# Softmax of a windowed attention: exponentials and sums taken for 512 columns at a time, on three engines

## The chip, the cores and the metric

The kernel runs on one core of a Trainium2 chip. The metric is device time in microseconds (us) of one execution. Five engines with a queue each work side by side: TensorE (PE, with its weight loads as PEld), VectorE (DVE), ScalarE (ACT), GpSimd (POOL) and SyncE (SP), which here issues all DMAs. Every queue runs in order.

## What is computed

```python
# q, k, v: (8, 8, 576, 64) float32
scores = np.matmul(q, k.transpose(0, 1, 3, 2)) / np.sqrt(64)
mask = (rel >= 0) & (rel < 64)           # rel: query position minus key position
scores = np.where(mask, scores, -1e9)
scores = scores - np.max(scores, axis=-1, keepdims=True)
attn = np.exp(scores)
attn = attn / (np.sum(attn, axis=-1, keepdims=True) + 1e-09)
x = np.matmul(attn, v)                   # turned to (4608 tokens, 512)
out = np.maximum(x @ w_in, 0) ** 2 @ w_out   # w_in (512, 2048), w_out (2048, 512)
```

## The kernel before

The 4608 tokens are cut into 12 tiles of 384. Each tile's attention is done in 3 **sections** of four blocks of 64 queries for two heads, 36 sections in all, numbered from 0. A section's scores lie as 128 partitions by 512 columns: eight groups of 64 columns, and each group is one softmax row per partition. The feed-forward part follows; with its high and low parts of every operand it is nearly all of the TensorE's work.

The function `section` (line 224) issues a section's steps; a letter names each:

- S: scores on TensorE (line 238). o: ScalarE copies one half of them to SBUF (line 246). s: VectorE puts the other half under the mask (lines 255, 256). z: VectorE takes the negated maxima of the eight groups (line 258).
- y: multiplies the eight maxima by the scale (line 260), on VectorE (`d`) or GpSimd (`p`).
- e and f: eight exponentials on ScalarE (line 266), four in each letter, of 64 columns each. The scale and, as bias, the group's negated maximum go with the instruction, and it also gives the group's sum; the profile shows each as an ACTIVATE and an ACTIVATION_READ_ACCUMULATOR.
- k: adds the epsilon to the sums (line 269). R: their reciprocals on VectorE (line 272). m: the probabilities times them, 128x512 (line 275), on GpSimd but for section 0.
- X: transposes on TensorE (line 279). x: VectorE masks them into SBUF (line 283). V: the product with v on TensorE (line 301). H and Q: high and low part of its result, on ScalarE (line 316) and VectorE (line 318).

The order of the instructions has two makers. The first ten sections (0 to 9) stand with all other work of their time in a list written out by hand, the string `order` (lines 491 to 510); a token is a letter, a number and, for some, an engine letter. Sections 0 to 5 lie at the kernel's start, 6 to 9 later. In the same string the steps a, b, c, d, h, l (`weight`, line 110) split one block of the weights into high and low part: a and h on ScalarE (lines 121, 132), b (two instructions, lines 123 and 124), c, d (lines 126, 128) and l (line 135) on VectorE. M (line 407), r and p (line 416 on), g, G (lines 424, 426) and O (line 449) are a feed-forward step: the first product, its evacuation and square, high and low part, the second product. T and U turn q and k on TensorE, t and u copy them, K fills TensorE with products of no use.

The 26 later sections are ordered by `Plan` (lines 655 to 723): each operation is given to it with an engine, a cost and what it reads and writes. TensorE's order is as written; the others are placed by when they are due. `weigh` (line 785) gives it the softmax:

```python
plan("dve", 0.68, by(section, "z", i), [sel], [nm])
plan("dve", 0.07, by(section, "y", i, "d"), [], [nm])
plan("act", 1.4, by(section, "e", i), [nm], [sel, sums])
plan("act", 1.4, by(section, "f", i), [nm], [sel, sums])
```

k and R follow there on VectorE and m on GpSimd; `cross` (line 817) plans X and x. Plain GpSimd work beside it is `mix` (lines 539, 543) and the squares (line 970).

## Time and profile before

| | |
|---|---|
| Three runs | 839.74, 839.88 and 840.94 us, median 839.88 |
| Span of the profiled execution, first to last instruction | 841.0 us; the page gives no other time for it |
| Busy share of the span | PE 98%, PEld 91%, VectorE 74%, ScalarE 52%, GpSimd 29% |
| Mean granted TensorE clock | 0.998 of full speed |

A page of the profile lists busy times, waits and the chain of work that ended last; the trace answers for a stretch, a line or an engine. Times in a timeline are us from the span's start. A matmul's duration is that of a pipelined instruction: matmuls overlap each other, so their busy sums, not their means, say what they take. An instruction on VectorE, ScalarE or GpSimd also overlaps the next one of its engine by up to a tenth of a us.

### The profile page before, as it was taken

The page shows a single profiled execution, that of the slowest core. Times are in us where ns is not written, and L with a number is a line of the kernel's source. Part 1 is how long each engine was busy: PE and PEld are TensorE (multiplying, and loading weights), DVE is VectorE, ACT ScalarE, POOL GpSimd, SP SyncE. Part 2 cuts the span into 40 slices and gives each one's busy share as a digit, 9 for nine tenths or more (in the row PEclk, how much of TensorE's full clock was granted, in tenths as well). Part 3 has the DMA queues.
Part 4 walks back from the last instruction along what each step waited for, and adds up shares of the span by engine and source line. Part 5 has one row for each costly group of instructions (what it writes and reads, how often), then busy time and mean ns, then how long its engine had stood idle before and what let it go on. Part 6 is the DMA issues. An engine that isn't in the chain of part 4 may idle for free.

```text
span 841.0 us, 18284 instructions
## 1 busy us (share of the span) xinstructions
PE 826.7 (98%) x6928; PEld 764.2 (91%) x6928; DVE 620.5 (74%) x908; ACT 435.2 (52%) x1181; POOL 242.7 (29%) x313
## 2 busy tenths in 40 slices
PE   8799999999999999999999999999999999999998
PEld 6689899889999999999999999999999999999997
DVE  5899998467666867867777866788766759566876
ACT  6796774655546554544452455444355424455441
POOL 1220003024547520221251334252233452202121
PEclk9999999999999999999999999999999999999999
DMA  9999964737588894999896897999895866789842
GB/s 211 223 321 301 288 272 80 146 101 183 148 196 258 219 186 101 308 258 215 184 315 211 219 229 169 252 292 223 275 309 140 262 202 192 244 269 310 243 167 76
DMA packets 292264, 184.99 MB, mean 220 GB/s; under 512 B 191184, under 2 KB 257488, under 8 KB 290128
## 3 DMA queue, kind: packets, MB, share of 16 engines
q1 hardware_dynamic: 292176, 183.81, 78.6%
q8 instruction: 55, 0.90, 0.5%
q14 instruction: 33, 0.27, 0.1%
HBM read 142.87 MB, written 40.89 MB: 219 GB/s over the span
## 4 chain that ended last, share of the span: by engine, by line
PE 90%; DVE 3%; SPq 3%; ACT 2%; issue 1%; DMA 1%; POOL 0%; ACTq 0%; POOLq 0%
PE banks L940 26%; PE banks L1038 24%; PE banks L449 13%; PE banks L407 13%; PE banks L1189 5%; PE banks L238 4%; PE banks L301 3%; PE banks L279 2%; SPq L160 1%; ACT a L121 1%; DVE a L126 1%; SPq L188 1%; DMA w<-in_k_dram 1%; ACT sel L266 1%; SPq L107 1%
## 5 line engine op out<-in xcount | busy, mean ns | idle before, releaser
L1038 PE MATMUL banks<-w 128*128 128x512 f32 x888 | 199.8, 381 | 0.0
L1038 PEld LDWEIGHTS banks<-w 128*128 128x128 f32 x888 | 165.9, 189 | 21.6
L407 PE MATMUL banks<-x,w 128*128 128x384 f32 x768 | 137.9, 329 | 0.4 <-ACT r L416 0.4
L449 PE MATMUL banks<-w,g 128*128 128x512 f32 x576 | 136.1, 382 | 0.0
L407 PEld LDWEIGHTS banks<-x,w 128*128 128x128 f32 x768 | 125.9, 189 | 5.7 <-ACT r L416 2.3
L940 PE MATMUL banks<-x,w 128*128 128x384 f32 x768 | 130.3, 326 | 0.0
L940 PEld LDWEIGHTS banks<-x,w 128*128 128x128 f32 x768 | 125.6, 189 | 0.0
L449 PEld LDWEIGHTS banks<-w,g 128*128 128x128 f32 x576 | 106.4, 189 | 13.3 <-issue 0.3
L266 ACT ACTIVATE sel<-sel,nm 128x64 f32<-128x64 f32 x272 | 90.8, 336 | 22.3 <-DVE nm L260 21.9
L940 PE MATMUL banks<-w 128*128 128x384 f32 x576 | 100.7, 329 | 0.0
L970 POOL TENSOR_TENSOR g<-g 128x384 f32<-128x384 f32 x48 | 46.5, 973 | 180.5 <-ACT g L981 172.6
L940 PEld LDWEIGHTS banks<-w 128*128 128x128 f32 x576 | 93.4, 189 | 1.6
L1045 DVE TENSOR_TENSOR w<-w,banks 128x512 f32<-128x512 f32 (+1 forms) x61 | 41.1, 677 | 41.3 <-PE banks L1038 41.2
L416 ACT ACTIVATE r<-banks 128x384 f32<-128x384 f32 x64 | 31.2, 487 | 65.3 <-PE banks L407 59.9
L275 POOL TENSOR_TENSOR sel<-sel,nm 128x512 f32<-128x512 f32 x33 | 37.3, 1131 | 81.9 <-ACT g L981 31.9
L539 POOL TENSOR_TENSOR a<-w 128x256 f32<-128x256 f32 x28 | 24.4, 887 | 104.9 <-DVE w L135 75.0
L426 DVE TENSOR_TENSOR g<-r,g 128x384 fp32r<-128x384 f32 x64 | 38.2, 600 | 21.3 <-ACT g L424 14.4
L1022 ACT CAST w<-w 128x512 fp32r<-128x512 f32 x37 | 23.0, 621 | 56.3 <-PE banks L1038 56.3
L266 ACT ACTIVATION_READ_ACCUMULATOR sel<-sel,nm 128x1 f32 x272 | 51.1, 188 | 0.0
L283 DVE TENSOR_TENSOR pt<-banks,masks 128x1024 f32<-128x1024 f32 x33 | 40.2, 1219 | 9.1 <-PE banks L279 9.1
L958 DVE TENSOR_TENSOR w<-banks,r 128x384 f32<-128x384 f32 x64 | 38.3, 598 | 11.7 <-PE banks L940 11.2
L421 DVE TENSOR_TENSOR r<-r 128x384 f32<-128x384 f32 x38 | 24.7, 650 | 26.3 <-ACT r L416 26.2
(167 smaller groups left out, 1273.4 us busy)
## 6 DMA issues: line engine op xcount, KB each, us to landing
w<-mixed SPq DMA_DIRECT2D x128, 256.0 KB, 5.6
w<-kept SPq DMA_DIRECT2D x114, 256.0 KB, 6.1
w<-kept SPq DMA_DIRECT2D x52, 512.0 KB, 7.3
kept<-w SPq DMA_DIRECT2D x16, 1024.0 KB, 8.7
vt<-in_v_dram SPq DMA_DIRECT2D x144, 64.0 KB, 3.7
w<-in_moe_w_in_dram SPq DMA_DIRECT2D x16, 512.0 KB, 7.7
w<-in_moe_w_out_dram SPq DMA_DIRECT2D x16, 512.0 KB, 7.8
raw<-in_q_dram SPq DMA_DIRECT2D x112, 72.0 KB, 2.9
```

What stands on the lines that cost most here:

```text
L266: act.activation(sels[i][:, w, hd], sels[i][:, w, hd], AF.Exp, bias=nms[i][:, n], scale=SCALE, accum_out=sums[i][:, n])
L275: (dve if eng == "d" else pool).tensor_tensor(p, p, rs[i][:, :, None].broadcast_to([P, SW * 2, QB]), ALU.mult)
L283: dve.tensor_tensor(pts[i].rearrange("p (w n) q -> p w n q", n=2), ps_t[i][:, :, None, :].broadcast_to([P, SW, 2, P]), masks.rearrange("p ...
L407: pe.matmul(h_ps, lhsT=weights(kk, part), rhs=in_turn(x[xx][:, kk // 2, kk % 2]), start=n == 0, stop=n == 3 * NK - 1)
L426: (pool if eng == "p" else dve).tensor_tensor(gs[n][1], rg.pop(n), gs[n][0].bitcast(F32), ALU.subtract)
L449: pe.matmul(acc(t, tb), lhsT=gg[:, tb * P:(tb + 1) * P], rhs=in_turn(weights(part)), start=f == 0 and n == 0, stop=f == NF - 1 and n == 2)
L940: pe.matmul(ps[:, :TT], lhsT=w[:, part, kk * P:(kk + 1) * P], rhs=in_turn(x[:, xx, kk]), start=n < 4 and m == 0, stop=m == 5, skip_group_c ...
L958: plan("dve", 0.6, lambda: dve.tensor_tensor(to(), ps, other(), ALU.add), [kps, ko], keys, 0, after)
L970: plan("pool", 0.95, lambda: pool.tensor_tensor(x(), x(), x(), ALU.mult), [], keys)
L1038: pe.matmul(ps[:, :DM // parted], lhsT=gg[:, m // 2, m % 2], rhs=in_turn(wo_slot(w[m])[:, part, cols]), start=m == 0 and n == 0, stop=m == ...
L1045: plan("dve", 0.72 / parted, lambda ps=ps, to=to: dve.tensor_tensor(by_half(to()), by_half(to()), ordered(ps[:, :DM // parted]), ALU.add), ...
L1189: pe.matmul(ps[:, x * 2 * P:(x + 1) * 2 * P], lhsT=gg[:, st, x * P:(x + 1) * P], rhs=in_turn(w[:, st, part]), start=c == 0, stop=c == 5, s ...
```

## The change

Three of a section's steps are made anew. y adds the negated maxima to all 512 columns, by an addition with a broadcast operand of the same shape as m's multiplication; in `order` all y stand on GpSimd now, and the planner is told GpSimd too. e is one exponential of 512 columns with the scale, without bias and without a sum. f is a sum over each group of 64 on VectorE, a reduction of the shape of z's. In `order` the tokens y0d and y1d become y0p and y1p, and for sections 2, 3, 4, 6, 7 and 9 the letters e and f change places, so that e stands first. The planner's costs change with the steps.

```diff
--- before.py
+++ after.py
@@ -257,14 +257,12 @@
         elif op == "z":
             dve.tensor_reduce(nms[i], sels[i].rearrange("p w h c -> p (w h) c"), AX.X, ALU.max, negate=True)
         elif op == "y":
-            (dve if eng == "d" else pool).tensor_scalar(nms[i], nms[i], SCALE, None, ALU.mult)
-        elif op in "ef":
-            for w in range(SW // 2):
-                w += "ef".index(op) * SW // 2
-                for hd in range(2):
-                    n = slice(2 * w + hd, 2 * w + hd + 1)
-                    act.activation(sels[i][:, w, hd], sels[i][:, w, hd], AF.Exp, bias=nms[i][:, n], scale=SCALE,
-                                   accum_out=sums[i][:, n])
+            p = sels[i].rearrange("p w h c -> p (w h) c")
+            (dve if eng == "d" else pool).tensor_tensor(p, p, nms[i][:, :, None].broadcast_to([P, SW * 2, QB]), ALU.add)
+        elif op == "e":
+            act.activation(sels[i], sels[i], AF.Exp, scale=SCALE)
+        elif op == "f":
+            dve.tensor_reduce(sums[i], sels[i].rearrange("p w h c -> p (w h) c"), AX.X, ALU.add)
         elif op == "k":
             (dve if eng == "d" else pool).tensor_scalar(sums[i], sums[i], EPS, None, ALU.add)
         elif op == "R":
@@ -489,11 +487,11 @@
             n1 += 1
     steps += [(0, f) for f in range(n0, NF)] + [(2, f) for f in range(LAG)]
     order = """
-        L0 K5 P0 L1 P1 T1 t1d T0 t0a J0 j0 Y0 S0 o0a T2 t2a s0 z0 y0d T3 t3d J1 L2 K2 S1 j1 e0 o1a T4 t4a v0 w1 Y1 L3 v1
-        N0 f0 K2 T5 d0 k0p t5a h0 s1 K5 z1 y1d S2 R0 m0d e1 l0 o2a X0 K5 x0 V0 s2 f1 k1p T6 R1 w2 z2 a1 b1 m1p X1 H0a Q0
-        c1 t6a v2 L4 N1 y2p K2 f2 T7 t7a x1 S3 e2 d1 U0 o3a s3 V1 k2p R2 u0a U1 z3 h1 u1a K5 H1a l1 Q1
-        m2p X2 x2 w3 v3 a2 b2 K3 c2 y3p f3 V2 T8 T9 H2a Q2 t8a t9a d2 S4 e3 o4a k3d R3 h2 s4 M0 U2 r0 u2a l2 p0a v4 z4
-        U3 u3a a3 m3p X3 x3 b3 g0 G0 M1 c3 r1 p1a y4p S5 o5a w4 v5 s5 d3 f4 e4 w5 w6 g1 G1 V3 H3a k4p R4 z5 Q3
+        L0 K5 P0 L1 P1 T1 t1d T0 t0a J0 j0 Y0 S0 o0a T2 t2a s0 z0 y0p T3 t3d J1 L2 K2 S1 j1 e0 o1a T4 t4a v0 w1 Y1 L3 v1
+        N0 f0 K2 T5 d0 k0p t5a h0 s1 K5 z1 y1p S2 R0 m0d e1 l0 o2a X0 K5 x0 V0 s2 f1 k1p T6 R1 w2 z2 a1 b1 m1p X1 H0a Q0
+        c1 t6a v2 L4 N1 y2p K2 e2 T7 t7a x1 S3 f2 d1 U0 o3a s3 V1 k2p R2 u0a U1 z3 h1 u1a K5 H1a l1 Q1
+        m2p X2 x2 w3 v3 a2 b2 K3 c2 y3p e3 V2 T8 T9 H2a Q2 t8a t9a d2 S4 f3 o4a k3d R3 h2 s4 M0 U2 r0 u2a l2 p0a v4 z4
+        U3 u3a a3 m3p X3 x3 b3 g0 G0 M1 c3 r1 p1a y4p S5 o5a w4 v5 s5 d3 e4 f4 w5 w6 g1 G1 V3 H3a k4p R4 z5 Q3
         h3 l3 a4 M2 r2 p2a O0 b4 O1 w7 v6 m4p X4 x4 c4 M3 g2 G2 V4 y5p e5 f5 k5p r3 H4a p3a g3 R5 d4 h4 a5 Q4
         w8 O2 G3 l4 m5p X5 x5 M4 a6 V5 w9 w10 w11 i3 r4 p4a g4 b6 H5d Q5 b5 M5 I3 r5 p5a c6 d6 w12 M6 w13 G4 O4
         h6 g5 r6 p6a c5 g6 M7 w14 d5 h5 w15 v7 v8 G5 O5 l6 r7 p7a a8 q0 M8 G6 O6 g7 l5 a7 r8 M9 b8 c8 d8 h8 G7 r9 O7
@@ -503,10 +501,10 @@
         B5 B6 B7 l12 G15 M17 r17 a14 p17a O15 M18 G16 O16 b13 c13 r18 M19 d13 b14 g17 G17 O17 c14 h13 p18a l13
         g18 G18 O18 d14 r19 M20 a15 p19a b15 g19 G19 h14 l14 r20 O19 c15 d15 p20a g20 M21 G20 B8 B9 D0 q2 O20 h15 l15 r21
         M22 p21a g21 G21 O21 D1 q3 r22 p22d g22 M23 r23 G22 O22 p23d M24 g23 G23 O23 Z22 S6 D2 q4 r24
-        p24d g24 G24 o6a M25 D3 s6 O24 S7 z6 r25 p25a g25 G25 M26 r26 p26d D4 y6p O25 M27 g26 W22 q5 G26 o7d O26 f6
-        e6 k6p R6 v9 s7 r27 p27a M28 q6 m6p r28 p28a z7 y7p f7 S8 g27 D5 q7 M29 X6 G27 O27 o8a x6 s8 z8 g28 V6
-        r29 v10 p29a g29 e7 M30 H6a G28 Q6 G29 S9 O28 k7p y8p e8 R7 m7p X7 o9d x7 r30 s9 p30d f8 k8p R8 m8p M31
-        r31 z9 y9p V7 g30 H7a Q7 G30 p31d g31 O29 X8 x8 O30 V8 f9 e9 G31 i31 k9p R9 m9p H8a Q8 D6 M32 r32 I31 Z31 v11
+        p24d g24 G24 o6a M25 D3 s6 O24 S7 z6 r25 p25a g25 G25 M26 r26 p26d D4 y6p O25 M27 g26 W22 q5 G26 o7d O26 e6
+        f6 k6p R6 v9 s7 r27 p27a M28 q6 m6p r28 p28a z7 y7p e7 S8 g27 D5 q7 M29 X6 G27 O27 o8a x6 s8 z8 g28 V6
+        r29 v10 p29a g29 f7 M30 H6a G28 Q6 G29 S9 O28 k7p y8p e8 R7 m7p X7 o9d x7 r30 s9 p30d f8 k8p R8 m8p M31
+        r31 z9 y9p V7 g30 H7a Q7 G30 p31d g31 O29 X8 x8 O30 V8 e9 f9 G31 i31 k9p R9 m9p H8a Q8 D6 M32 r32 I31 Z31 v11
         W31 D7 p32d g32 X9 M33 x9 G32 r33 p33d g33 G33 q8 q9"""
     ps_f = {}
 
@@ -789,9 +787,9 @@
         plan("act", 0.56, by(section, "o", i), ["s_ps"], [sel])
         plan("dve", 0.73, by(section, "s", i), ["s_ps"], [sel])
         plan("dve", 0.68, by(section, "z", i), [sel], [nm])
-        plan("dve", 0.07, by(section, "y", i, "d"), [], [nm])
-        plan("act", 1.4, by(section, "e", i), [nm], [sel, sums])
-        plan("act", 1.4, by(section, "f", i), [nm], [sel, sums])
+        plan("pool", 1.13, by(section, "y", i, "p"), [nm], [sel])
+        plan("act", 0.65, by(section, "e", i), [], [sel])
+        plan("dve", 0.68, by(section, "f", i), [sel], [sums])
         if i in loads:
             b, part = divmod(loads[i], len(VPARTS))
             if b < B:
```

## Rows read from the trace of the kernel before

**Rows 1.** The page's first part: busy us (share of the span) xinstructions of each engine.

```profile
PE 826.7 (98%) x6928; PEld 764.2 (91%) x6928; DVE 620.5 (74%) x908; ACT 435.2 (52%) x1181; POOL 242.7 (29%) x313
```

**Rows 2.** Windows: busy us (xinstructions) of PE, PEld, DVE, ACT, POOL; PEclk; DMA; GB/s.

```profile
20.00:30.00 10.00, 6.30 (x133) 4.96 (x134) 8.40 (x12) 7.56 (x27) 4.14 (x6) 0.99 0.81 211
30.00:40.00 10.00, 9.01 (x124) 8.37 (x123) 8.13 (x11) 7.33 (x25) 0.03 (x1) 0.84 1.00 217
40.00:50.00 10.00, 9.21 (x126) 8.46 (x126) 9.57 (x14) 9.42 (x29) 1.59 (x4) 1.00 0.98 287
50.00:60.00 10.00, 8.71 (x92) 7.51 (x91) 9.58 (x13) 9.78 (x27) 4.38 (x4) 1.00 1.10 324
80.00:90.00 10.00, 10.00 (x54) 9.00 (x53) 9.83 (x13) 8.03 (x12) 0.00 (x0) 1.00 0.58 103
200.00:330.00 130.00, 130.00 (x1217) 119.80 (x1216) 90.33 (x143) 69.03 (x227) 62.35 (x92) 1.00 0.77 191
31.00:32.00 1.00, 1.00 (x7) 1.00 (x6) 0.65 (x1) 1.00 (x2) 0.00 (x0) 0.50 1.11 166
```

**Rows 3.** Waits of PE, whole span: us in total, times, longest us.

```profile
PE banks L279 <- POOL sel L275: 1.3, 1, 1.3
PE banks L301 <- DVE pt L283: 1.2, 2, 0.6
...
PE banks L407 <- ACT r L416: 0.4, 1, 0.4
```

**Rows 4.** Groups by line, each form apart: busy us, mean ns of one, idle before.

```profile
L266 ACT ACTIVATE sel<-sel,nm 128x64 f32<-128x64 f32 x272 | 90.8, 336 | 22.3 <-DVE nm L260 21.9 <-POOL nm L260 0.2
L266 ACT ACTIVATION_READ_ACCUMULATOR sel<-sel,nm 128x1 f32 x272 | 51.1, 188 | 0.0
...
L258 DVE TENSOR_REDUCE nm<-sel 128x8 f32<-128x512 f32 x34 | 23.0, 678 | 0.7
...
L1022 ACT CAST w<-w 128x512 fp32r<-128x512 f32 x37 | 23.0, 621 | 56.3 <-PE banks L1038 56.3
...
L123 DVE TENSOR_SCALAR a<-a 128x1024 f32<-128x1024 f32 x15 | 10.8, 720 | 1.6 <-ACT a L121 1.6
...
L275 DVE TENSOR_TENSOR sel<-sel,nm 128x512 f32<-128x512 f32 x1 | 0.7, 691 | 0.0
```

**Rows 5.** Timeline of POOL: start us, us, instruction, idle before it and releaser.

```profile
21.27 1.04 POOL L275 TENSOR_TENSOR sel<-sel,nm 128x512 f32<-128x512 f32 x1 [0.32 <-DVE nm L272]
...
29.40 0.24 POOL L260 TENSOR_SCALAR nm<-nm 128x8 f32<-128x8 f32 x1
...
50.91 1.21 POOL L260 TENSOR_SCALAR nm<-nm 128x8 f32<-128x8 f32 x1
...
56.87 2.02 POOL L275 TENSOR_TENSOR sel<-sel,nm 128x512 f32<-128x512 f32 x1 [0.39 <-DVE nm L272]
...
176.28 1.04 POOL L275 TENSOR_TENSOR sel<-sel,nm 128x512 f32<-128x512 f32 x1 [4.04 <-DVE nm L272]
```

**Rows 6.** Timeline of DVE, 20 to 60 us.

```profile
21.79 1.08 DVE L123 TENSOR_SCALAR a<-a 128x1024 f32<-128x1024 f32 x1
...
30.42 1.23 DVE L135 TENSOR_TENSOR w<-a,w 128x1024 fp32r<-128x1024 f32 x1 [1.48 <-ACT w L132]
...
50.81 1.21 DVE L135 TENSOR_TENSOR w<-a,w 128x1024 fp32r<-128x1024 f32 x1
...
53.31 1.22 DVE L283 TENSOR_TENSOR pt<-banks,masks 128x1024 f32<-128x1024 f32 x1
...
56.63 1.36 DVE L128 SCALAR_TENSOR_TENSOR a<-w,a 128x1024 int32<-128x1024 int32 x1
```

**Rows 7.** Timeline of PE, around 55 us and at 178 us.

```profile
54.59 0.93 PE L301 MATMUL banks<-pt,vt 64*64 64x64 f32 x48
...
58.94 0.65 PE L279 MATMUL banks<-ident,sel 128*128 128x128 f32 x4 [1.29 <-POOL sel L275]
...
178.04 0.63 PE L279 MATMUL banks<-ident,sel 128*128 128x128 f32 x4
```

## The prediction

> **What bounds the kernel now.** I read the page's first part before anything else: TensorE is busy for 826.7 us of 841.0, so at most 841.0 - 826.7 = 14.3 us can be won by anything that TensorE waits for, however much a softmax shrinks on another engine [rows 1]. The question is then where these 14.3 us lie, and the windows answer it. From 200 to 330 us TensorE is busy 130.00 of 130, while VectorE has 90.33 and ScalarE 69.03: a burst of sections there costs nothing, and relief of ScalarE there gives nothing. At the start it is otherwise: TensorE has 6.30, 9.01, 9.21 and 8.71 of 10 in the four windows from 20 to 60 us, and from then on 10.00 again [rows 2]. The list of waits says what it waits for there: the transposes X wait 1.3 us once for GpSimd's m, V 1.2 us in all for VectorE's x, and a product once 0.4 us for ScalarE [rows 3].
>
> So the start decides, and there sections 0 to 5 share their engines with the splitting of the weights. Look at who is full: from 40 to 60 us VectorE has 9.57 and 9.58, ScalarE 9.42 and 9.78. VectorE stays at 9.83 from 80 to 90, where ScalarE has fallen to 8.03 [rows 2]. Two full engines alternate on the chain; the change unloads one and loads the other.
>
> **The change, part by part.** The sum is made against the profiled execution: 841.0 us from first to last instruction, the only time that the page gives for it, 1.1 above the median 839.88 of the three runs. I work out a difference and add it to the median.
>
> *Exponentials.* Eight activations of 64 columns with accumulator reads go. They take between 8 x 0.336 = 2.7 us, if the reads hide behind the next activation, and 8 x (0.336 + 0.188) = 4.2 us if they do not. The new one is not in the trace; the nearest row is a ScalarE operation of 512 columns, 0.62 us, the bounds are 0.34 (one of 64 columns) and 0.69 (VectorE's price for 512) [rows 4]. I take 0.62: ScalarE wins 2.1 to 3.6 us a section. What is that worth? Only where TensorE waits for ScalarE, 0.4 us in all [rows 3], or where VectorE waits for it.
>
> *Sums.* f is a reduction of z's shape, 0.68 us [rows 4]: six sections before 60 us, 6 x 0.68 = 4.1 us more in VectorE's queue. Room there is the idle time from 20 to 60 us: 1.60 + 1.87 + 0.43 + 0.42 = 4.3 us [rows 2], of which the largest piece is 1.48 us ahead of a weight step [rows 6]. About 0.4 of it are waits inside a softmax that stay, since k still stands on GpSimd behind the sum; I take 3.9. By itself the reduction would nearly fit, were it spread as the idle time is. It is not: of the 4.3 only 0.85 lie behind 40 us, where f3 to f5 need 3 x 0.68 = 2.0, so 1.2 us is what the sums alone cost.
>
> *Subtractions on GpSimd.* y grows from 0.24 us to the shape of m, 1.04 us [rows 5]. Its own length is the smaller part. Look at the two engines side by side. At 50.91 a GpSimd y of eight columns takes 1.21 us in place of 0.24, and it ends at 52.12, just behind VectorE's weight step that runs from 50.81 to 52.02. At 56.87 an m takes 2.02, beside a VectorE step that runs to 57.99: 0.98 more. At 21.79 it goes the other way: VectorE's b takes 1.08 us in place of 0.72, beside an m that began first, at 21.27, and ends at 22.31 [rows 4 to 6]. Whichever began first holds the other off. So a subtraction of 1.04 us can hold up VectorE for 1.04 us where its next step is a weight step or m.
>
> The Trainium skill states this as a rule (SBUF — State Buffer, "SBUF: two separate sides"): GpSimd and VectorE share one port pair under an exclusive lock for a whole instruction, when VectorE runs a 2-port mode or has two SBUF inputs. By it the sum below holds, without it the second rival's; this trace agrees, with the 1.21 and 2.02 us above.
>
> I go through the queues in the new order. y0 starts when z0 ends; a copy from PSUM passes it, then a half b waits some 0.4 us. y1 starts when z1 ends, R0 passes, and m0 waits some 0.9 us. y2 stands behind m1 on GpSimd and slips in between the two instructions of b1: 1.04. Everything is then so late that m2 meets l1: 0.65. y3 and y4 fall beside Q and x steps, which read PSUM and one SBUF operand; no row shows these held up, so I take zero, with 1.04 each as the bound. y5 waits for l3, as before, but then takes its turn before b4: 1.04. Together 0.4 + 0.9 + 1.04 + 0.65 + 1.04 = 4.0 us; the bounds are zero and 6 x 1.04 + 0.65 = 6.9.
>
> *The start's sum.* VectorE gets 4.1 + 4.0 us and has 3.9 of room: its step l4 and section 5's m come 4.2 us later. Who waits? V of section 4 stands right behind x (x ends at 53.31 + 1.22 = 54.53, V starts at 54.59), and X of section 5 right behind m (56.87 + 2.02 = 58.89, X at 58.94) [rows 5 to 7]. There is no slack, and behind them TensorE has no idle time to take the delay up [rows 2]. Moving the two old y off VectorE gives back too little to count.
>
> The skill's GPSIMD Engine Reference (4.1, Engine selection) also speaks against y: two-input elementwise work is about twice as slow there as on VectorE, which with VectorE's 0.69 would make 1.4 us an estimate for y and the sum above some 0.3 us longer for each y that holds VectorE. The row of the same shape says 1.04 [rows 5], a factor of 1.5, and decides.
>
> *Sections 6 to 9.* In section 8 f stands between p30 and R in VectorE's queue, where R once followed at once: 0.68 for f and some 0.4 for k on GpSimd and the two hand-overs, 1.1 us. m ended at 176.28 + 1.04 = 177.32 and X starts at 178.04 [rows 5, 7], so 0.7 are slack and 0.4 us is lost. The other three have longer cover or a shorter chain.
>
> *The 26 planned sections* I cost at nothing. A section's chain loses 2.1 or more on ScalarE and gains 0.9 on GpSimd and 0.7 on VectorE; VectorE, 90.33 of 130, and GpSimd, 62.35 of 130, have room for it [rows 2]. The cover is the time between a section's m and its X; where a collision takes it away, that section costs up to 1 us, and a new order by the planner's new costs can bring more such places.
>
> *The clock.* TensorE's granted clock is 0.50 from 31 to 32 us, its lower level of 1.2 GHz, after a window in which it was busy 6.30 of 10; the window 30 to 40 has 0.84, which is 1.6 us lost of 10 [rows 2]. The later arrival of V1 and X1 may fill that idle time, and new waits of about 2 us ahead of V4 and X5 may open another. I take zero and keep 1.6 us for either end.
>
> Sum: 4.2 + 0.4 = 4.6, so 839.9 + 4.6 = 844.5 us.
>
> **Rivals.** *ScalarE was the bound.* The time between two VectorE steps at 40 to 56 us could be ScalarE's: it has 9.42 and 9.78 of 10 there. Then sections 4 and 5 come early by 2.1 us each, X5's 1.3, V's 1.2 and the 0.4 us wait vanish [rows 3], and the time is 839.9 - 2.9 = 837.0. The point from which it decides: VectorE would have to have 2 us of room from 40 to 60, and has 0.85. Chance 0.14.
>
> *The collisions cost little*, because VectorE's steps happen to fall otherwise than in my walk. Then the sums' 1.2 and section 8's 0.4 are left, less what the clock gives back: 839.9 + 1.6 = 841.5 at most, and about 841 as its centre. For it: y3 and y4 already cost nothing in my count. Against it: weight steps fill VectorE's queue in this stretch, and b, d and l are the very ones that show a collision in the rows [rows 5, 6]. Chance 0.22.
>
> *The middle breaks too.* Ten of the later sections lose 0.4 us each, as section 8 does: 844.5 + 4 = 848.5. For it: GpSimd at half its time in the window from 200 to 330. Against it: TensorE waits for nothing there. Chance 0.08, within slower.
>
> **How the numbers follow.** About 0.2% (1.7 us) is what a measurement of this kernel can tell from no change: 838.2 to 841.6. Forecast 0.56 and the third rival 0.08 make slower 0.64; the second rival makes same 0.22, the first faster 0.14. The forecast's own bounds: with no collision 841.5; with all of them 4.1 + 6.9 - 3.9 = 7.1, + 0.4 + 1.6 = 9.1, so 849.0. The range goes from 839.0 to 849.0: its low end takes in the second rival even where the clock gives all its 1.6 back (839.9), and a last us for my walk through the queues; left out are the first rival and what lies above.
>
> **What would show it.** Right: VectorE at 9.8 or more of 10 from 20 to 60 us; b1, m0 and b4 longer by about a subtraction; X5 at about 63 us with a wait for GpSimd of 2 us; no wait of TensorE behind 200 us; ScalarE's busy time down by 36 x 2.1 = 76 us or more without a gain. Wrong: X5 at or before 59 us, no longer weight steps beside y, or waits of TensorE in the middle.

## The result and the profile after

The changed kernel takes 851.31 us in the median of four runs (850.3 to 852.55), beside 839.87 (839.74 to 840.94) for the kernel before on the same chip: a ratio of 1.0132 with a 95% interval of 1.0118 to 1.0146. It is slower, as forecast, but by 11.4 us where 4.6 were forecast, and it lies above the range.

The page's first part for the changed kernel, in the columns of [rows 1]:

```profile
PE 828.6 (98%) x6928; PEld 765.0 (90%) x6928; DVE 639.5 (75%) x916; ACT 363.4 (43%) x641; POOL 279.7 (33%) x341
```

ScalarE does 71.8 us less than before, VectorE 19.0 more, GpSimd 37.0 more. The span is 848.7 us, 7.7 longer: TensorE stands idle for 20.1 us where it was 14.3, which is 5.8 of them, and its own busy time is 1.9 longer. (The span of before is that of an untypical execution, as shown below; a typical one is some 3 us shorter.)

The windows of the changed kernel, in the columns of [rows 2]:

```profile
20.00:30.00 10.00, 6.56 (x136) 5.24 (x138) 9.61 (x13) 4.54 (x7) 2.96 (x4) 1.00 0.90 219
30.00:40.00 10.00, 7.67 (x133) 6.80 (x123) 9.93 (x13) 5.05 (x8) 3.92 (x3) 0.80 0.93 215
40.00:50.00 10.00, 9.54 (x121) 8.81 (x122) 8.24 (x13) 7.44 (x14) 2.08 (x2) 0.86 1.03 308
50.00:60.00 10.00, 9.02 (x93) 8.10 (x92) 9.84 (x13) 5.84 (x9) 3.50 (x3) 1.00 1.10 324
60.00:70.00 10.00, 8.17 (x87) 6.88 (x86) 9.18 (x14) 6.37 (x9) 2.15 (x2) 1.00 1.06 375
200.00:330.00 130.00, 128.07 (x1206) 117.90 (x1206) 92.28 (x143) 52.72 (x107) 75.79 (x107) 1.00 0.80 189
```

Set against [rows 2], VectorE is full in three of the four windows from 20 to 60 us, ScalarE is far from full in all of them, TensorE now also idles in the window behind 60, and the stretch from 200 to 330 us, which had none, now has 1.93 us. In this execution TensorE's clock also fell: it has 0.50, the level of 1.2 GHz, from 36 to 42 us, behind a wait of 1.49 us ahead of section 2's V. At half its clock it came to the transposes X3 at 44.72 us (42.52 in the repeat of this kernel, **after_again** below, whose clock is 1.00 there), and VectorE's next x waited 1.66 us for them: that is why VectorE has 8.24 in the window behind. The wait alone does not tell when the clock falls: the repeat has the same 1.49 us ahead of the same V.

The list of waits of the changed kernel (us in total, times, longest), answering to [rows 3]; L277 is X, L299 is V, L405 a feed-forward product, L273 is m, L281 is x, L414 is r:

```profile
PE banks L277 <- POOL sel L273: 3.2, 2, 1.8
PE banks L299 <- DVE pt L281: 3.2, 4, 1.5
PE banks L405 <- ACT r L414: 2.5, 3, 1.9
...
PE banks L277 <- DVE sel L273: 1.3, 1, 1.3
...
PE banks L299 <- DVE w L281: 1.0, 1, 1.0
PE banks L277 <- POOL w L273: 0.8, 1, 0.8
PE banks L199 <- DMA w<-in_k_dram: 0.5, 1, 0.5
```

The three waits of [rows 3] are there again, and each is longer: 3.2 for 1.3, 3.2 for 1.2, 2.5 for 0.4. The first two belong to the start, but for 0.25 us of section 8's V. The longest of the third is new: it is the 1.93 us behind 200 us. The next three lines are waits of the start for m and x that the list of before doesn't have. The last one is shorter than before: TensorE turns q and k at the start, and it waited 3.2 us in all for transfers of the operand k in the profiled execution of before, 0.5 here.

The new operations, from the groups of the changed kernel:

```profile
L263 ACT ACTIVATE sel<-sel 128x512 f32<-128x512 f32 x34 | 21.4, 629 | 28.3 <-POOL sel L261 28.3
L265 DVE TENSOR_REDUCE nm<-sel 128x8 f32<-128x512 f32 x34 | 23.0, 677 | 1.4 <-ACT sel L263 1.3
```

An exponential of 512 columns takes 0.63 us (0.62 was taken) and a sum 0.68 (0.68). No price of one operation was far off.

### The walk through the queues, held against the trace

GpSimd's timeline of the changed kernel (start, us, line, idle before and its releaser): the subtractions y are L261.

```profile
11.71 1.04 POOL L261 TENSOR_TENSOR sel<-sel,nm 128x512 f32<-128x512 f32 x1 [8.05 <-ACT a L121]
...
17.40 1.04 POOL L261 TENSOR_TENSOR sel<-sel,nm 128x512 f32<-128x512 f32 x1 [1.35 <-DVE nm L258]
...
24.17 1.49 POOL L261 TENSOR_TENSOR w<-w,nm 128x512 f32<-128x512 f32 x1
...
32.68 2.02 POOL L261 TENSOR_TENSOR w<-w,nm 128x512 f32<-128x512 f32 x1
...
43.90 1.04 POOL L261 TENSOR_TENSOR sel<-sel,nm 128x512 f32<-128x512 f32 x1 [1.82 <-DVE nm L258]
...
54.18 2.03 POOL L261 TENSOR_TENSOR sel<-sel,nm 128x512 f32<-128x512 f32 x1
```

VectorE's timeline, the steps that stand beside them (b is L123 and L124, m0 is L273, l is L135):

```profile
12.04 0.99 DVE L123 TENSOR_SCALAR a<-a 128x512 f32<-128x512 f32 x1
...
17.46 1.53 DVE L273 TENSOR_TENSOR sel<-sel,nm 128x512 f32<-128x512 f32 x1
...
24.80 1.42 DVE L124 TENSOR_SCALAR a<-a 128x1024 int32<-128x1024 int32 x1
...
32.09 1.72 DVE L135 TENSOR_TENSOR w<-a,w 128x1024 fp32r<-128x1024 f32 x1
...
55.22 1.53 DVE L123 TENSOR_SCALAR a<-a 128x1024 f32<-128x1024 f32 x1
```

The same steps take 0.42, 0.69, 0.69, 1.23 and 0.69 us where nothing holds them (from the timelines of this and the other kernels). They are longer by 0.57, 0.84, 0.73, 0.49 and 0.84, together 3.5 us; 0.4, 0.9, 1.04, 0.65 and 1.04 were forecast, at these five places. (The l is held by an m in an undisturbed start of the old kernel too, b_planned_new below, where it takes 1.65 us, so some 3.0 of the 3.5 are new, and the forecast's 0.65 at this place was no loss of the change.) The y at 32.68, once the l is done, and the y at 43.90 hold nobody up, also as forecast; at 43.90 VectorE had nothing to do, but in the repeat, where that y stands beside an x, the x takes its usual 1.21 us. The Trainium skill's rule (SBUF — State Buffer, "SBUF: two separate sides": whichever engine begins first has the port pair for its whole instruction) agrees with these rows: y at 17.40 began 0.06 us ahead of m0, and m0 ends 0.55 us behind its end, so that most of m0's own 0.69 came after it; at 54.18 VectorE's l began first, at 54.09, and y took 2.03 in place of 1.04.

And section 5's X, TensorE's timeline:

```profile
63.49 0.33 PE L277 MATMUL banks<-ident,sel 128*128 128x128 f32 x1 [1.75 <-POOL sel L273]
```

58.94 plus 4.2 was forecast, about 63, with a wait of 2 us for GpSimd. It looks like a hit. It is not, as the next part shows: 58.94 was the wrong place to start from.

### The profile page after: what moved, and what is told of

The parts are those of the page before. It is cut to its first block, busy times and chain, and to the rows that moved or that the text cites. A ratio compares the mean times of both kernels' runs of the same rounds, so it can differ in the third digit from the quotient of the medians.

```text
span 848.7 us, 17786 instructions
## 1 busy us (share of the span) xinstructions
PE 828.6 (98%) x6928; PEld 765.0 (90%) x6928; DVE 639.5 (75%) x916; ACT 363.4 (43%) x641; POOL 279.7 (33%) x341
## 4 chain that ended last, share of the span: by engine, by line
PE 83%; DVE 7%; SPq 5%; DMA 2%; issue 1%; ACT 1%; POOL 1%; DVEq 0%; POOLq 0%
PE banks L938 26%; PE banks L1036 24%; PE banks L405 10%; PE banks L447 10%; PE banks L1187 5%; PE banks L238 3%; PE banks L299 3%; SPq L160 2%; PE banks L277 1%; DVE a L126 1%; SPq L150 1%; DVE a L128 1%; DVE w L135 1%; SPq L188 1%; SPq L738 1%
## 5 line engine op out<-in xcount | busy, mean ns | idle before, releaser
L405 PE MATMUL banks<-x,w 128*128 128x384 f32 x768 | 139.4, 332 | 2.5 <-ACT r L414 2.5
L405 PEld LDWEIGHTS banks<-x,w 128*128 128x128 f32 x768 | 127.2, 191 | 8.1 <-ACT r L414 4.9
L261 POOL TENSOR_TENSOR sel<-sel,nm 128x512 f32<-128x512 f32 x34 | 37.4, 1099 | 191.4 <-DVE nm L258 154.4
L414 ACT ACTIVATE r<-banks 128x384 f32<-128x384 f32 x64 | 31.3, 489 | 79.6 <-PE banks L405 72.4
L281 DVE TENSOR_TENSOR pt<-banks,masks 128x1024 f32<-128x1024 f32 x33 | 40.2, 1217 | 8.6 <-PE banks L277 8.6
L273 POOL TENSOR_TENSOR sel<-sel,nm 128x512 f32<-128x512 f32 x33 | 37.4, 1134 | 23.6 <-DVE nm L270 19.7
L170 DVE STREAM_TRANSPOSE qk<-raw 128x1152 f32<-128x1152 f32 x28 | 38.2, 1367 | 5.7 <-PE banks L238 3.3
```

Of the source, the lines that this page charges most:

```text
L170: dve.transpose(get_turned(b, g // 2)[:, g % 2].rearrange("p n t -> p (n t)"), raw.rearrange("p n t -> p (n t)"))
L261: (dve if eng == "d" else pool).tensor_tensor(p, p, nms[i][:, :, None].broadcast_to([P, SW * 2, QB]), ALU.add)
L281: dve.tensor_tensor(pts[i].rearrange("p (w n) q -> p w n q", n=2), ps_t[i][:, :, None, :].broadcast_to([P, SW, 2, P]), masks.rearrange("p ...
L405: pe.matmul(h_ps, lhsT=weights(kk, part), rhs=in_turn(x[xx][:, kk // 2, kk % 2]), start=n == 0, stop=n == 3 * NK - 1)
```

## The experiments

All times are medians on the chip; the kernel before ran beside each batch of kernels, at 840.09, 840.02, 840.6 and 840.33 us. Those named a_... are made from the changed kernel, those named b_... from the kernel before. X5 is the start of section 5's first X, in each run's profile. TensorE executes the same 6928 instructions in the same order in all these kernels, so one instruction's start can be set against itself.

### Which half of the sections loses the time

**a_planned_old**: sections 0 to 9 in the new form and order, the 26 planned ones in the old form with the old costs.

```diff
+            if i < 10:
...
-        plan("pool", 1.13, by(section, "y", i, "p"), [nm], [sel])
-        plan("act", 0.65, by(section, "e", i), [], [sel])
-        plan("dve", 0.68, by(section, "f", i), [sel], [sums])
+        plan("dve", 0.07, by(section, "y", i, "d"), [], [nm])
+        plan("act", 1.4, by(section, "e", i), [nm], [sel, sums])
+        plan("act", 1.4, by(section, "f", i), [nm], [sel, sums])
```

> Sections 0 to 9 as changed, sections 10 to 35 in the old form with the planner's old costs. Theory (the start and the hand-ordered sections make some 5.5 us, one wait of 1.9 us near 323 us comes from the planner's new order): span 848.7 - 1.9 = 846.8 us, no wait of TensorE behind 200 us, X of section 5 still at 63.5 us. Rival (that wait is a late DMA, whatever the order): the wait is there again and the span stays at 848.7.

Measured: 847.78 us (847.03 to 848.42), ratio 1.0094 (1.0079 to 1.0109). The theory holds for the planned part: behind 200 us the list of TensorE's waits is empty. X5 is at 62.23, with the clock at 1.00 throughout, so 1.26 us of the 63.49 belong to the drop of the clock in the changed kernel's first profile.

**b_planned_new**: the complement, sections 0 to 9 old, the planned ones new with the new costs.

> The complement: sections 0 to 9 in the old form and order, sections 10 to 35 changed with the new costs. Theory: the start as before (X of section 5 at 58.9 us), and one wait of about 1.9 us for ScalarE's r near 315 us, behind a ScalarE copy that waits for a DMA; span 841.0 + 1.9 = 842.9 us. Rival (the planned sections cost nothing by themselves and the wait only follows from the late start): 841.0 us, no wait behind 100 us.

Measured: 842.55 us (840.8 to 844.67), ratio 1.0029 (1.0018 to 1.0040). So the first ten sections lose 7.7 us and the planned ones 2.5; together 10.2, about what the whole change loses (9.8 and 11.4 in its two series). Its profile is that of the fastest of ten executions (840.8 us, span 839.0 for 842.9 expected), and its one wait for r is of 0.49 us where 1.9 were expected: no trace shows the median's 2.5.

This run also has the kernel before's start in an execution without a late transfer (its longest wait for the operand k is 0.6 us). Its windows:

```profile
20.00:30.00 10.00, 8.66 (x151) 6.89 (x152) 9.58 (x13) 8.77 (x29) 3.79 (x6) 1.00 0.91 226
30.00:40.00 10.00, 7.43 (x124) 6.54 (x123) 9.79 (x15) 8.48 (x27) 1.62 (x2) 1.00 0.86 227
40.00:50.00 10.00, 10.00 (x126) 9.18 (x125) 9.64 (x14) 9.51 (x27) 2.70 (x4) 1.00 1.02 334
50.00:60.00 10.00, 8.64 (x134) 7.38 (x132) 9.25 (x12) 9.67 (x27) 2.26 (x2) 1.00 1.11 325
```

and its X5:

```profile
56.20 0.33 PE L287 MATMUL banks<-ident,sel 128*128 128x128 f32 x1 [1.29 <-POOL sel L283]
```

The instructions here are those of [rows 2], yet X5 starts 2.7 us earlier than there. VectorE idles 1.7 us from 20 to 60, not 4.3, and the clock is 1.00 throughout, where [rows 2] has 0.84 from 30 to 40. The profiled execution of before was an untypical one. A transfer of the operand k came late in it, TensorE waited 2.0 us for it at 26.3, and the clock fell behind that wait:

```profile
28.27 0.55 PE L199 MATMUL banks<-ident,w 128*128 128x128 f32 x3 [1.99 <-DMA w<-in_k_dram]
```

Three waits of VectorE right behind this one, 1.48 us for l, 0.42 for Q and 0.92 for x, are not in the other start: they made most of its idle time.

The two starts also give the loss of the first ten sections without the clock. Scores of a later section (L238) start at 257.66 us in a_planned_old and at 250.72 in b_planned_new: 6.94 us, of which X5 has 6.03. The fastest run of a_planned_old, the profiled one with a clock of 1.00, took 847.03 us; its other three have a mean granted clock of 0.996 and took 0.3 to 1.4 us more.

### What loses the start's time

**b_extra_sum**: the kernel before with one more reduction of 512 columns on VectorE in each of the sections 0 to 5, of data that nobody uses, at f's place.

```diff
+            if i < 6 and op == ("f", "f", "e", "e", "e", "f")[i]:
+                dve.tensor_reduce(dsum, dum, AX.X, ALU.add)
```

> The kernel before, with one VectorE reduction of 128x512 where f stands after the change in each of sections 0 to 5, on a tile that nothing else needs. Theory (the sums fit where VectorE idles up to 40 us and not behind it): X of section 5 about 1.2 us later, span 842.2. Rival one (they fit everywhere): 841.0. Rival two (VectorE's queue sets the start all along): 6 x 0.65 = 3.9 later, 844.9.

Measured: 842.61 us (842.1 to 843.47), ratio 1.0033 (1.0021 to 1.0045), X5 at 58.46. X5 comes 2.26 us later than the 56.20 above, between the theory's 1.2 and the second rival's 3.9; the first rival falls.

**b_extra_sub**: the kernel before with one more addition of m's shape on GpSimd in each of these sections, at y's place.

```diff
+            if i < 6:
+                pool.tensor_tensor(dum, dum, nms[i][:, :, None].broadcast_to([P, SW * 2, QB]), ALU.add)
```

> The kernel before, with one GpSimd addition of 128x512 behind y in each of sections 0 to 5, on a tile that nothing else needs. Theory (GpSimd holds VectorE off): VectorE's instructions beside it grow by up to 1.04 us each, X of section 5 comes 1.5 to 3 us later than 58.9, span 842.5 to 844. Rival (the subtraction costs only as a link of the softmax's chain): nobody waits for these, span 841.0 within 0.3.

Measured: 841.99 us (841.24 to 843.0), ratio 1.0019 (1.0009 to 1.0029). The time is 1.9 us over before, and the rival falls. X5 stands at 58.70, 2.5 us later, in an execution with a drop of the clock (0.78 from 36 to 42 us), so the split of the 2.5 is open; VectorE's busy time, below, is the better witness.

**b_extra_both**: both loads at once.

> The kernel before with both loads at once in sections 0 to 5: a GpSimd addition and a VectorE reduction of 128x512 each, on tiles that nothing else needs. Theory (load on VectorE and the held-off port pair are nearly all of the start's loss): the two loads alone made 1.9 and 2.5 us, together at least 4.4 us over before, X of section 5 at 60.5 us or later. Rival (the links y, f and k in the softmax's chain, which nothing here lengthens, make the larger part): X of section 5 before 59.5 us.

Measured: 843.9 us (843.56 to 844.61), ratio 1.0046 (1.0031 to 1.0061), X5 at 60.82: by X5 the theory holds, and the time is 3.9 us over before, where it had at least 4.4. Loads that change nothing in the old softmax's chain push X5 by 4.6 us, where the change does it by 6.1 (62.34 in the repeat below, 62.23 in a_planned_old). Some 0.4 of the 4.6 are not the loads': a transfer of weights came later in this execution, and section 0's z starts at 11.41 us, where the old start and the repeat have it at 10.97. So the loads make 4.2 of 6.1.

**after_again**: the changed kernel once more, beside the next one.

> The changed kernel as it is, beside the others on one chip. Its time was 11.4 us over the kernel before on another chip; with 7.7 us for the start and the hand-ordered sections and 2.5 us for the planned ones, as the two halves measured, 10.2 us over before are expected here, and again one wait for ScalarE's r of 1 to 4 us near 320 us.

Measured: 849.85 us (847.33 to 851.18), ratio 1.0112 (1.0092 to 1.0132), 9.8 over before, X5 at 62.34, and a wait of 2.17 us for r at 320. This execution too had a drop of the clock, to 0.86 from 20 to 30 us, but its X5 is within 0.11 us of a_planned_old's.

**a_no_sub**: the changed kernel without the subtraction in sections 0 to 5 (the maxima are found there and not subtracted).

```diff
+            if i >= 6:
```

> The changed kernel without the subtraction in sections 0 to 5 (the exponentials take the scores as they are). Theory (GpSimd's 512-column subtractions hold VectorE off and stand in the chain): VectorE's b1, m0 and b4 at their old durations, X of section 5 some 3 us earlier than with it, near 59.5 us, the time about 3 us below the changed kernel. Rival one (VectorE's queue with the six sums is all): less than 1 us. Rival two (the subtractions are all): X of section 5 at 56.2 us, as in an execution of the old start without a late DMA.

Measured: 847.72 us (845.51 to 848.14), ratio 1.0084 (1.0067 to 1.0101), 2.1 below the changed kernel, where the theory had about 3 and the first rival less than 1; the two intervals overlap a little. Its profile is of an execution in which the operand k came late (one wait of 1.97 us), with X5 at 60.94, so X5 tells less here than VectorE's busy time does.

That busy time, from 10 us to each run's own X5, is the shortest way to read these runs together. The third number behind the window's length is VectorE's, the fourth ScalarE's. First the old start (b_planned_new):

```profile
10.00:56.20 46.20, 40.14 (x573) 34.63 (x571) 44.45 (x63) 41.80 (x139) 10.61 (x14) 1.00 0.97 260
```

The old start with the six reductions (b_extra_sum):

```profile
10.00:58.46 48.46, 40.42 (x573) 34.94 (x572) 47.92 (x69) 42.06 (x139) 12.10 (x14) 1.00 0.98 260
```

With the six additions on GpSimd (b_extra_sub):

```profile
10.00:58.70 48.70, 40.99 (x574) 35.57 (x573) 46.49 (x63) 42.08 (x139) 18.27 (x20) 0.96 0.97 260
```

With both loads (b_extra_both):

```profile
10.00:60.82 50.82, 41.50 (x574) 35.85 (x575) 50.34 (x70) 42.39 (x139) 20.13 (x20) 1.00 0.91 238
```

The changed kernel (after_again):

```profile
10.00:62.34 52.34, 41.47 (x574) 35.84 (x572) 50.99 (x67) 30.25 (x49) 17.84 (x16) 0.97 1.03 277
```

The same first ten sections at full clock (a_planned_old):

```profile
10.00:62.23 52.23, 40.28 (x574) 34.57 (x572) 50.97 (x67) 30.39 (x49) 17.83 (x16) 1.00 0.99 265
```

Without the subtractions (a_no_sub):

```profile
10.00:60.94 50.94, 41.19 (x575) 35.36 (x573) 47.66 (x67) 29.98 (x49) 9.17 (x10) 0.97 0.99 257
```

VectorE has 44.45 of 46.20 us in the old start: 1.75 us of room. The change takes it to 50.99, 6.54 more, and leaves 1.35 idle, so 0.4 of the room was used and X5 comes 6.54 - 0.40 = 6.14 us later. That the change runs through GpSimd shows in b_extra_sub: VectorE executes 63 instructions as in the old start, no other step reads what the additions write, and VectorE is busy 2.0 us longer.

The last fence splits the 6.54: without the subtractions it is 47.66, so the sums, less the two old y that left VectorE, cost 47.66 - 44.45 = 3.2 us, and the subtractions, which run on another engine, cost VectorE 50.99 - 47.66 = 3.3 us of longer instructions. The split is good to some 0.4 us: in a_no_sub's late execution the l beside m2 began after m2 and took 1.23 us, while in the old start m2 holds it (1.65); with that put right the subtractions cost 2.9, beside the 3.0 of the walk. ScalarE loses 11.5 us of work in the same stretch, and X5 comes no earlier for it.

Counted from section 0's z, 2.0 us lie between b_extra_both and the repeat (49.41 and 51.37 us to X5): 1.2 are VectorE's busy time, 50.16 for 48.96 (the useless additions met its steps at other places), and 0.8 its idle time. For the idle part there was a suspect, the way from f over k on GpSimd back to R:

**a_k_dve**: the changed kernel with k of sections 0, 1, 2, 4 and 5 on VectorE.

```diff
- ... f0 K2 T5 d0 k0p ...
+ ... f0 K2 T5 d0 k0d ...
```

> The changed kernel with k (the epsilon) of sections 0, 1, 2, 4 and 5 on VectorE, where f and R stand already, instead of GpSimd. Theory (what the start loses beyond the two added loads, 62.3 less 60.8 us at section 5's X, is the way from f over GpSimd to R, where R waits some 0.35 us a time and one k took 1.14): X5 starts 0.7 to 1.5 us earlier, at 60.8 to 61.7, and the time is 848.4 to 849.2, 0.7 to 1.5 below the changed kernel's 849.9. Rival (R's wait only shows time that VectorE then loses elsewhere): X5 at 62 or later, time within 0.5 of 849.9.

Measured: 849.39 us (849.2 to 849.52), ratio 1.0099 (1.0083 to 1.0116), X5 at 62.17. The rival held at X5: VectorE's idle time falls to 52.17 - 51.55 = 0.6 us, and the five k take the 0.6 us themselves. The time cannot tell: 849.39 is 0.5 below the repeat, but it was taken beside another series of before, and the two ratios overlap. Here the wait within a full engine's chain was no gain, since what removed it is work on that engine.

**a_no_max**: the changed kernel without z and y in all sections (no maximum is found or subtracted), k on VectorE as above. VectorE's load is then that of the old start.

```diff
-            dve.tensor_reduce(nms[i], sels[i].rearrange("p w h c -> p (w h) c"), AX.X, ALU.max, negate=True)
+            pass
```

> The changed kernel without z and y in all 36 sections: the maxima are neither found nor subtracted, and k stands on VectorE in sections 0, 1, 2, 4 and 5. This leaves out the reference's subtraction of the row maximum. VectorE then loses z, 0.68 us, for f, 0.68, and GpSimd's subtractions are gone. Theory (the change loses by VectorE's added work and by the subtractions that hold it off): X5 starts at 56.5 or earlier and the time is 837.5 to 840.5, unless a wait of the planned part adds up to 2. Rival (the start is set by something else than VectorE's load, such as the length of one section's chain through four engines): X5 at 59 or later, time 842 or more.

Measured: 843.08 us (842.35 to 845.55), ratio 1.0030 (1.0019 to 1.0041), X5 at 58.60. It falls between the two expectations at X5, and by its time on the rival's side. VectorE has 45.98 us busy from 10 us to X5, 1.5 more than the old start, since m meets weight steps otherwise (the l at 49.47 takes 1.82 us where its like in the old start took 1.22, the one at 29.38 takes 1.93 for 1.65), and it idles 0.9 us more, in waits for ScalarE's weight steps. The profile is again not of an undisturbed start: TensorE waited 0.72 us for the operand k, and the clock was 0.50 from 24 to 26 us; how much of X5 that is, is open. So it is not shown that VectorE's sum of work is all: which step a GpSimd instruction falls on moves the start by a us or more.

**b_no_max**: the kernel before without z and y in sections 0 to 5 (there no maximum is found or subtracted), else unchanged.

```diff
+        elif op in "zy" and i < 6:
+            pass
...
-act.activation(..., AF.Exp, bias=nms[i][:, n], scale=SCALE,
+act.activation(..., AF.Exp, bias=nms[i][:, n] if i >= 6 else 0.0, scale=SCALE,
```

> The kernel before without z and y in sections 0 to 5: the maxima are neither found nor subtracted there, the eight exponentials of a section have no bias; all else is as before. This leaves out the reference's subtraction of the row maximum in those sections. Theory (VectorE's load sets the time of the start): six reductions less, 6 x 0.66 = 4.0 us, bring X5 from 56.2 to between 52.5 and 54.5, and the time falls by 1.7 to 3.7 us, to 836.5 to 838.5. Rival (at the old load another engine is next, ScalarE with 9.84 of 10 from 40 to 50 us): X5 at 55.2 or later and less than 1 us won.

Measured: 839.75 us (838.48 to 841.49), ratio 0.9992 (0.9982 to 1.0001), X5 at 54.81. Between the two again. Six reductions less bring X5 by 1.4 us, where six more pushed it by 2.3 (b_extra_sum), and VectorE, at 41.66 of 44.81, now idles 3.2 us, of which 1.2 is one wait for k on GpSimd and 0.8 waits for ScalarE's weight steps. So more work on VectorE lengthens the start, while less work on it soon meets waits for other engines.

### What loses time in the planned sections

In the changed kernel the wait behind 200 us is this one, on TensorE:

```profile
323.19 1.08 PE L405 MATMUL banks<-x,w 128*128 128x384 f32 x5 [1.93 <-ACT r L414]
```

and on ScalarE the queue ahead of that r:

```profile
322.13 0.62 ACT L543 CAST a<-a 128x512 fp32r<-128x512 f32 x1 [5.72 <-DMA mixed<-a]
322.66 0.48 ACT L414 ACTIVATE r<-banks 128x384 f32<-128x384 f32 x1
```

A copy of a mix (L543) waits 5.72 us until a DMA has read its buffer, and r, which TensorE needs, stands behind it. In the repeat TensorE waited 2.17 us here, and its granted clock was 0.83 in the window from 320 to 330. b_planned_new has the same wait of ScalarE, 4.85 us at 312.52, and there 0.49 us of it reached TensorE. The planner placed the copy there by its new costs: with the old ones (b_planned_order below) this wait is not there. Three runs, made from b_planned_new, tried to tell the order from the work itself.

**b_planned_lands**: the planner is told that a mix's write lands after 9.0 us instead of 4.5.

```diff
-        plan("sp", 0.55, by(mix, "F", h), [mx], [("mixed", h // 2, h % 2)], 4.5, (), 1.4)
+        plan("sp", 0.55, by(mix, "F", h), [mx], [("mixed", h // 2, h % 2)], 9.0, (), 1.4)
```

> Old sections 0 to 9, changed sections 10 to 35, and the planner told that the writes of the mixed weights land 9.0 us after their issue in place of 4.5, so that ScalarE's copy of the next mix stands one r later. Theory (a ScalarE copy that waits for such a write holds up r behind it, by an amount that varies from run to run): no wait of TensorE for r behind 100 us, time within 0.7 us of before, and a narrower spread than the 840.8 to 844.7 us without it. Rival (GpSimd's load or VectorE's sums cost the 2.5 us): time stays 2 us over before.

Measured: 847.44 us (846.56 to 848.08), ratio 1.0086 (1.0071 to 1.0101). The wait for r is gone, and elsewhere there is a longer one, on TensorE:

```profile
294.04 0.87 PE L287 MATMUL banks<-ident,sel 128*128 128x128 f32 x3 [4.46 <-ACT a L324]
```

whose cause is on ScalarE, an exponential (L266) that waits for y with the copy H of V's result (L324) behind it:

```profile
292.79 0.63 ACT L266 ACTIVATE sel<-sel 128x512 f32<-128x512 f32 x1 [5.18 <-POOL sel L262]
293.33 0.57 ACT L324 COPY a<-banks 128x512 f32<-128x512 f32 x1
```

Neither expectation had this. The clock is 0.66 from 290 to 300 us.

**b_planned_cost**: the planner is told 2.8 us for the exponential, what the eight cost before.

```diff
-        plan("act", 0.65, by(section, "e", i), [], [sel])
+        plan("act", 2.8, by(section, "e", i), [], [sel])
```

> The kernel before in sections 0 to 9, the changed form in the 26 planned ones, as in the run that did this alone and came out 2.5 us above the kernel before (842.55 beside 840.02 to 840.09). Here the planner is told 2.8 us for the exponential, as much as the eight cost it before, instead of 0.65, so that it places ScalarE's copies of the mix elsewhere. Theory (the planned sections cost time only where a copy of a mix, ahead of an evacuation r in ScalarE's queue, waits for a DMA): TensorE has no wait for r over 0.5 us behind 200 us and the time is 839.4 to 841.0. Rival (the planned sections' extra work on VectorE and GpSimd costs time by itself): 842 or more, with waits of TensorE for VectorE or GpSimd behind 200 us.

Measured: 843.14 us (842.35 to 847.56), ratio 1.0036 (1.0023 to 1.0050). The theory's sign and the rival's time: the copy's wait costs TensorE only 0.23 us now, but X waits for m on GpSimd twice, 0.53 us at 231 and 0.89 at 561.

**b_planned_order**: the new form with all the old costs and engines in the plan, so that the list of operations keeps the old order.

```diff
-        plan("pool", 1.13, by(section, "y", i, "p"), [nm], [sel])
-        plan("act", 0.65, by(section, "e", i), [], [sel])
-        plan("dve", 0.68, by(section, "f", i), [sel], [sums])
+        plan("dve", 0.07, by(section, "y", i, "p"), [], [nm])
+        plan("act", 1.4, by(section, "e", i), [nm], [sel, sums])
+        plan("act", 1.4, by(section, "f", i), [nm], [sel, sums])
```

> The kernel before in sections 0 to 9, the changed form in the 26 planned ones, but the planner is given the old costs and engines (a scaling of 0.07 us on VectorE, two exponentials of 1.4 us on ScalarE), so that every queue keeps the order it had before; only the work itself is new. Theory (the 2 to 3 us that the planned sections lost in the two earlier runs come from the planner's new order, which puts some step ahead of one that is due sooner): no wait of TensorE over 0.5 us behind 200 us, time within 0.7 of the kernel before, 839.9 to 841.3. Rival (they come from the work: GpSimd's subtraction and VectorE's sum make m late): TensorE waits for GpSimd's m or VectorE's x behind 200 us, time 842 or more.

Measured: 841.6 us (840.54 to 843.97), ratio 1.0012 (0.9998 to 1.0027), between the two expectations. In its profile one wait over 0.5 us is left, 0.65 for a step of VectorE's at 537.8. The likeliest reading is that the new order makes about half of the 2.5 us and the work the rest; the two intervals overlap, so the split is not shown. What is shown is that the waits sit at other places with each order, and that the two long ones, 1.93 and 4.46 us, are each on a step that stands behind one that is not ready.

No version ran faster than the kernel before by more than can be told: b_no_max, which leaves the maxima of six sections out, is 0.6 us below it, with an interval that reaches past 1.

## Why the forecast had the right sign and the wrong size

**What bounds the start: right.** VectorE, with GpSimd holding it off. The first rival (ScalarE) fell: 11.5 us of ScalarE's work left the start and nothing came early. The second fell too: the collisions cost 2.9 to 3.3 us.

**Exponentials: right.** 0.63 for 0.62 us. ScalarE's busy time fell by 71.8 us, where 76 or more were named: 2.0 us a section, at the lower bound of 2.1, in which the reads hide behind the next activation.

**Sums: 3.2 for 4.1 us.** Neighbours on VectorE overlap by some 0.1 us, so six reductions of 0.68 fill 3.47 us (47.92 - 44.45), not 4.1, and two y of old left. **Collisions: 2.9 to 3.3 for 4.0 us**, at the places named; one of them, m2 on l, was there before the change. By the factor of two that the Trainium skill gives for two-input work on GpSimd (GPSIMD Engine Reference, 4.1 Engine selection) y would take 1.4 us, an estimate (twice VectorE's 0.69). The measurement decides: where nothing holds it, y takes the 1.04 that the row said.

**Room: the step that failed.** "Room there is the idle time from 20 to 60 us: 1.60 + 1.87 + 0.43 + 0.42 = 4.3 us ... I take 3.9." Of it 0.4 us was used. The 4.3 belonged to one execution in which a transfer came late and VectorE waited with everyone else; in an undisturbed one there are 1.75 us from 10 us to X5. Loads outside the softmax's chain used 1.2 to 1.3 of these (0.54 and 0.48 are left in b_extra_sum and b_extra_both); the changed kernel, with new waits of its own, used 0.4. With 0.4 in place of 3.9 the forecast's own terms make 4.1 + 4.0 - 0.4 = 7.7 at the start, and with the measured terms 3.2 + 3.3 - 0.4 = 6.1. The forecast's terms with this one put right give 839.9 + 7.7 + 0.4 = 848.0, within its range; the planned sections' 2.5, below, lead to 850.5. That these come out so near is in part luck, since sums and collisions were taken 1.6 us too high: measured terms alone, 6.1 + 0.8 + 2.5, make 849.3, beside 849.85 and 851.31 in the two series.

**The base: wrong by the same cause.** The text set the span, 841.0, against the median of the times and found it 1.1 above. In all runs that show both, the time is 1.7 to 2.0 us longer than the span (850.6 and 848.7, 840.8 and 839.0, 838.5 and 836.8). So a median run of before has a span of about 838.1, and the profiled one was 3 us longer than typical, of which its start has 2.7 (X5 at 58.94 for 56.20). Of 66 runs of before beside the experiments, 6 have a mean granted clock of 0.998 or less, as the profiled execution has. The list of TensorE's waits said so too: its first line, above those that [rows 3] quotes, is

```profile
PE banks L199 <- DMA w<-in_k_dram: 3.2, 3, 2.0
```

and the forecast took the lines below it for what TensorE waits for. That was the sign to ask what in this execution was not typical: the granted clock of 0.50 was already in [rows 2], and the text weighed it as 1.6 us of clock, and not as a mark that the idle time around it was not the kernel's own.

**X5 at 63 came out for the wrong reason**: a start 2.7 us too late (58.94 for 56.20) and a delay 1.9 too short (4.2 for 6.14), with 1.15 us more in the first profile, where the clock fell. Two errors of opposite sign met: luck.

**Sections 6 to 9: 0.4 forecast, 0.8 measured.** From 170 to 180 us TensorE's delay in a_planned_old, set against b_planned_new, grows from 6.14 to 6.94 us. The wait named for section 8 is there, X8 with 0.38 us; GpSimd's m ended at 183.01 us and VectorE's Q at 183.03, so either alone would have held X8 up. V behind it loses another 0.25, which was not in the sum.

**The planned sections: nothing forecast, 2.5 us measured** (842.55 beside 840.09), the second step that failed. "TensorE waits for nothing there" and the room on each engine were right; what the room does not show is that each queue runs in order. The third rival named ten losses of 0.4 us and a chance of 0.08; it is in part what happened, though as one or two waits of up to 2 us and not many small ones, at steps that the planner's new costs moved. That such waits make the whole 2.5 us is argued and not shown: the one trace of these sections alone has 0.5 us of it. Of the forecast's signs of being wrong, waits of TensorE in the middle, this one came.

**The clock: zero taken, 1.6 kept.** That it would neither gain nor lose did not hold: all eight runs of the changed kernel have a mean granted clock of 0.996 to 0.998, where 60 of the 66 runs of before have 0.999 or more. What a drop costs differs with its place. The one from 36 to 42 us in the first profile cost 1.26 us at X5, the one from 20 to 30 us in the repeat next to nothing there, and behind the wait at 320 it cost the repeat about 2 us. The runs of the changed kernel spread from 847.33 to 852.55 us over both series, and the two longest have 0.997 and 0.998, not the lowest: the mean clock does not order them, and the 1.5 us between the two medians stay open.

## What to carry to other kernels

Before idle time in one profile is used as room, find out whether that execution is a typical one: set its time beside the median, and look in its waits for a late transfer or a clock drop upstream of the idle time. An operation given to GpSimd was not free for VectorE here: it was paid on VectorE, by 0.6 to 0.8 us of its 1.04, wherever that engine's next step was one that it holds off, and this could be walked through beforehand, place by place. Relief on an engine that TensorE didn't wait for bought nothing, and a planner that was told of it put a waiting step ahead of an urgent one.

## Not expected of the hardware

- The time is 1.7 to 2.0 us longer than the span from first to last instruction, in every run here that shows both.
- A GpSimd instruction of eight columns, 0.23 us alone, took 1.14 us at 14.91 and at 29.76 beside a weight step of VectorE: a held instruction paid for the other's length, however small it was itself.
- One and the same wait of TensorE is followed by a lower clock in some executions and not in others. The 1.49 us ahead of section 2's V stand in ten of the traces here; the granted clock fell to 0.50 behind it, the level of 1.2 GHz, in the changed kernel's first profile (36 to 42 us) and in b_extra_sub, and stayed at 1.00 in the other eight.
- Where it falls, a wait can cost about its own length again. Behind the 1.93 us at 321 in the first profile the clock stayed at 1.00; behind the 2.17 us at 320 in the repeat it was 0.83 from 320 to 330, and the stretch from TensorE's instruction at 273.43 to the one at 339.69 took 66.25 us, where a_planned_old has 62.14 for it: 4.1 us for a wait of 2.17.
